# Attention scores of two head-pair units per pass over the TensorE array, and a new order of the steps of the first attention and of chunk 0

## The chip, the cores and the metric

One core of a Trainium2 chip runs the kernel. The metric is the time of one execution on the device in microseconds, the median over several runs. The engines are TensorE (PE, with its weight loads shown apart as PEld), VectorE (DVE), ScalarE (ACT), GpSimd (POOL) and SyncE (SP), which here only issues DMAs. Every engine works through its own queue in program order, and waits on semaphores for the others.

## What is computed

```python
scores = scale * q @ k.T                       # B=4, H=8, S=576, D=64
scores = where(mask[h], scores, -1e9)          # heads 0-3: window of 32; heads 4-7: window of 32 with stride 4
attn = exp(scores - max); attn /= sum + 1e-9
x = (attn @ v) as [2304, 512]
g = h - tanh(h),  h = x @ w_in                 # 512 -> 2048
x = g @ w_out                                  # 2048 -> 512
logits = x @ phi                               # 32 slots, 8 experts
slots = softmax over the tokens(logits).T @ x
out = softmax over the slots(logits) @ experts(slots)   # relu(slots @ w1) @ w2
```

## The kernel before, in words

The 2304 tokens are worked off in chunks of 512, `ch` 0 to 3, and a rest of 256. Each batch `b` of the attention gives the 512 tokens of chunk `b` and 64 of the rest.

**Attention.** The eight heads are four pairs (`PO = (2, 3, 0, 1)`: the two pairs with stride come first); each pair has three units `i`, so a batch has `NU = 12`. A unit holds two heads: head 0 in partitions 0 to 63 of q and k, head 1 in 64 to 127. A unit of a pair with stride has four blocks of 48 queries by 80 keys for each head, one of a plain pair three blocks of 64 by 96. A unit goes through `emit_scores` (PE: for batches 0 and 1 a bf16 matmul that writes the mask, then one f32 matmul for each block and head; DVE: the maximum, `L360`; ACT: the exponentials with their sums, `L363`), `emit_norm` (DVE: reciprocal, `L377`; POOL: the product, `L378`), `emit_trans` (PE: transposes, `L387`; ACT copies them out), `emit_pv` (PE: the product with v, `L408`; ACT copies the high part to `xhi`; DVE subtracts for the low part `xlo`, `L444`). An f32 matmul stands as two records in the trace, so the 84 score matmuls of a batch's 12 units are 168 records.

**Order.** The first attention (batch 0) runs alone, in an order that is sorted by numbers: unit `i` has the time `t = t0 + dt * i`, and its norm, transposes and product with v are put at `t` plus `NORM`, `TRANS` and `PV` times `dt`. The times only sort; nothing waits for them. Between the units stand conversions of weights, loads, and small `warm` matmuls. The attention of batch `b+1` is laid between the matmuls of chunk `b`, two units to a step.

**Chunk 0.** `mixed_step` runs eight times, `s` = 0 to 7. A step holds two blocks of 128 hidden columns, `a = 2s` and `b = 2s + 1`; each is twelve matmuls of 512 columns (`emit_h`, `L563` to `L565`), `tanh` on ACT (`L569`), the subtraction on DVE (`L572`), a transpose on DVE (`emit_gT`, `L585`) and logits on PE (`L578`). Between them the step converts further weights from 64-bit words (`conv_a` ACT `L496`; `conv_b` DVE `L504` and `L505`; `conv_in_c` ACT copy and POOL `L518`; `conv_out_c` PE `L526`, copies on ACT and DVE; `conv_out_d` PE `L537` and a copy on DVE to `cvb`), and carries the attention of batch 1 (`an`): `turn_qk` transposes a pair's q and k on DVE (`L260`, `L261`), in steps 0, 1, 2 and 4 (`QKS`), then `norms`, `trans`, `score`, `values`. The PSUM tiles `mm` are a ring of five; a PE group that takes one waits until the copy out of the tile five before it is done.

**Chunks 1 to 3** run `phase_step`, which has no conversions; chunks 1 and 2 carry batches 2 and 3, whose mask is added on DVE (`L357`). Then come the rest chunk, the slots, the experts and the output.

Of the kernel before, what the change touches and what calls it, by code (L numbers as in the profile page):

```python
# [31 lines left out]
MASKPE = 2  # L32
PO = (2, 3, 0, 1)
VB = (1, 2, 3)
# [10 lines left out]
NORM = (0.57, 0.28)  # L45
TRANS = (1.67, 1.76)
PV = (3.37, 3.39)
# [17 lines left out]
def moe_kernel(ctx: ExitStack, tc: tile.TileContext, q, k, v, w_in, w_out, phi, w1, w2, out):  # L65
# [258 lines left out]
    def emit_scores(b, i):  # L324
        p, u = PO[i // 3], i % 3
        nb, nq, nk = shape(i)
        ps = mm([128, nb, nk])
        mask = mask_d[:, (0, 4, 2)[u]:(4, 8, 6)[u]] if nb == 4 else mask_p[:, min(u, 1):min(u, 1) + 3]
        by_pe = b < MASKPE
        nr = nq if by_pe else 64  # L330
        if by_pe:
            nc.tensor.matmul(
                ps.rearrange("p c k -> p (c k)"), lhsT=id2.rearrange("p a k -> p (a k)"),
                rhs=mask[0:64].rearrange("p c k -> p (c k)"), start=True, stop=True,
            )
        for c in range(nb):
            for x in range(2):
                step = 1
                if nb == 4:

                    r2, qi = divmod(2 * u + c // 2, 3)
                    q0 = 288 * (c % 2) + 144 * r2
                    q0, k0 = q0 + nq * qi, q0 + max(0, nq * qi - 32)
                    if b in VB:
                        q0, k0 = (288 * (c % 2) + r2 + 2 * (t - 288 * (c % 2) - 144 * r2) for t in (q0, k0))
                        step = 2
                else:
                    q0, k0 = nq * (nb * u + c), max(0, nq * (nb * u + c) - 32)
                r = slice(64 * x, 64 * x + 64)
                nc.tensor.matmul(  # L350
                    ps[64 * x:64 * x + nr, c, :], lhsT=qT[b, p][r, q0:q0 + step * (nr - 1) + 1:step],
                    rhs=kT[b, p][r, k0:k0 + step * (nk - 1) + 1:step],
                    start=not by_pe, stop=True, skip_group_check=True,
                )
# [37 lines left out]
    def emit_pv(b, i):  # L392
# [5 lines left out]
        pt = sc_pt.pop((b, i))  # L398
        o = mm([128, 192])
        for n0 in range(nb):  # L400
            for hh in range(2):
                if nb == 4:
                    m, x = divmod(n0, 2)
                    r2, qi = divmod(2 * u + m, 3)
                    n, c, col = 3 * (2 * r2 + x) + qi, 2 * m + hh, 96 * x + nq * m
                else:
                    n, c, x, col = nb * u + n0, n0, hh, nq * n0
                nc.tensor.matmul(  # L408
                    o[64 * hh:64 * hh + 64, col:col + nq], lhsT=vt[b, p](n, hh),
                    rhs=pt[:, c, 64 * x:64 * x + nq], start=True, stop=True,  # L410
                )
# [34 lines left out]
        if b in VB:  # L446
            lows.append(low)
        else:
            low()
# [367 lines left out]
    class Attn:  # L817
# [19 lines left out]
        def score(self, i):  # L837
            if i < NU:
                emit_scores(self.b, i)
# [28 lines left out]
    with tc.manual_schedule():  # L868
# [7 lines left out]
        for b, (t0, dt) in enumerate((ATT0,)):  # L876
            for i in range(NU):
                t = t0 + dt * i
                at(t, emit_scores, b, i)
                at(t + NORM[b] * dt, emit_norm, b, i)  # L880
                at(t + TRANS[b] * dt, emit_trans, b, i)
                at(t + PV[b] * dt, emit_pv, b, i)
                if b == 0:
                    at(t + WAT * dt, warm, WARM if i < NWARM else 2)
            for p in range(NP):
# [5 lines left out]
        for t, f, *args in ((46.0, load_qk_blocks, 1, PO[0]), (50.0, load_v, 1, PO[0], nc.sync)):  # L891
            at(t, f, *args)
# [21 lines left out]
        for _, _, f, args in sorted(steps, key=lambda s: s[0:2]):  # L914
            f(*args)

# [13 lines left out]
        def mixed_step(an, ch, s, xh, xl, gs, posts):  # L930
# [7 lines left out]
            pa, gs[a] = emit_first(ch, xh, xl, a, first), gring.next()  # L938
            an.norms(s - 1)
            if 0 < s < 7:  # L940
                conv_a("in", 2 + a)
                conv_a("in", 2 + b)
            emit_tanh(pa, gs[a])
            if s == 0:
                conv_a("in", 2)
                conv_a("in", 3)
# [28 lines left out]
            an.score(2 * s)  # L975
            an.score(2 * s + 1)
# [10 lines left out]
        def phase_step(an, ch, s, xh, xl, gs, posts):  # L987

            a, b = 2 * s, 2 * s + 1
            pa, gs[a] = emit_h(xh, xl, a), gring.next()  # L990
            if an and s in QKS:
# [18 lines left out]
            if an:  # L1010
                an.trans(s)
                an.score(2 * s)
                an.score(2 * s + 1)
# [228 lines left out]
```

## Time and profile before

| | |
|---|---|
| median of 3 runs | 470.75 us (470.69 to 472.73) |
| profiled execution | 471.14 us, of which the trace spans 469.3 us |
| mean granted clock of TensorE in it | 0.976 of full speed |
| busy in the span: PE, DVE, ACT, POOL | 432.2, 250.8, 203.4, 83.8 us |
| first attention | about 5 to 62 us of the span |
| chunk 0 (`mixed_step`) | about 62 to 160 us |
| chunks 1 and 2 with batches 2 and 3 | about 160 to 310 us |

The trace gives, for each engine, when each group of instructions began, how long it took, how long the engine stood idle before it and on what. "mm<-qk 64*64 64x96" is a matmul into the tile `mm` from the tile `qk` with a 64 by 64 stationary and a moving operand of 64 partitions by 96 columns. A granted clock of 1.00 is 2.4 GHz, 0.50 is 1.2 GHz.

### The profile page before, as it was taken

To read this page: it belongs to the slowest core of one execution; us is meant where nothing else is said; L and a number is where in the kernel's file an instruction comes from. 1 tells how busy PE (TensorE), PEld (TensorE's weight loads), DVE (VectorE), ACT (ScalarE), POOL (GpSimd) and SP (SyncE) were. 2 spreads that over 40 slices of the span, in tenths; PEclk is the share of its full clock that TensorE was granted. 3 is DMA by queue.
4 is the path that set the end of the run, shared out by engine and by line. 5 is a ranking of instruction groups with operands and counts; after the bars stand their busy time and mean duration, and the time that the engine had idled before them with its cause. 6 is when DMAs were issued, how large, how long until landed. Compare 5 with 4: busy or idle time off the path is not lost.

```text
span 469.3 us, 11363 instructions
## 1 busy us (share of the span) xinstructions
PE 432.2 (92%) x4567; PEld 315.6 (67%) x4567; DVE 250.8 (53%) x605; ACT 203.4 (43%) x701; POOL 83.8 (18%) x99
## 2 busy tenths in 40 slices
PE   6989877999898999999999999999999999999980
PEld 4766646877677775887775788776777689645330
DVE  1455658578965775756475776453644251233041
ACT  4777436677664272654253455322212223213131
POOL 3321414334235040223031031100000000010000
PEclk9999899799999999999999999999999999999996
DMA  8998986889564202163423111167000799899938
GB/s 235 232 264 232 288 119 219 216 257 266 187 118 82 55 14 41 45 84 52 85 54 54 39 40 24 68 226 314 1 1 17 253 352 400 327 403 410 407 123 314
DMA packets 102021, 81.16 MB, mean 173 GB/s; under 512 B 78032, under 2 KB 81872, under 8 KB 101968
## 3 DMA queue, kind: packets, MB, share of 16 engines
q1 hardware_dynamic: 101968, 80.43, 57.6%
q8 instruction: 36, 0.59, 0.5%
q14 instruction: 17, 0.14, 0.1%
HBM read 71.50 MB, written 8.91 MB: 171 GB/s over the span
## 4 chain that ended last, share of the span: by engine, by line
PE 61%; issue 12%; DVE 11%; ACT 10%; DMA 3%; POOL 0%; DVEq 0%; SPq 0%; ACTq 0%; POOLq 0%
PE h L563 11%; PE h L564 10%; PE h L565 10%; PE mm L350 5%; PE lg L578 4%; PE mm L408 4%; ACT mem L363 3%; PE h L786 3%; PE y L811 3%; PE mm L702 3%; PE mm L387 2%; ACT mem L569 1%; DMA wo_dram<-cva 1%; DVE cva L505 1%; PE warm L205 1%
## 5 line engine op out<-in xcount | busy, mean ns | idle before, releaser
L563 PE MATMUL h<-xhi,wts 128*128 128x512 f32 x256 | 106.8, 417 | 0.4 <-ACT xhi L103 0.4
L564 PE MATMUL h<-xlo,wts 128*128 128x512 f32 x256 | 101.4, 396 | 0.0
L565 PE MATMUL h<-xhi,wts 128*128 128x512 f32 x256 | 100.9, 394 | 0.0
L569 ACT ACTIVATE mem<-h 128x512 f32<-128x512 f32 x72 | 42.9, 596 | 122.9 <-PE h L565 115.5
L572 DVE TENSOR_TENSOR mem<-h,mem 128x512 f32<-128x512 f32 x72 | 49.4, 686 | 86.5 <-ACT mem L569 86.4
L378 POOL TENSOR_TENSOR mem<-mem 128x320 f32<-128x320 f32 (+1 forms) x48 | 33.3, 703 | 169.9 <-DVE mem L377 108.6
L563 PEld LDWEIGHTS h<-xhi,wts 128*128 128x128 f32 x256 | 49.1, 192 | 16.5 <-issue 5.9
L565 PEld LDWEIGHTS h<-xhi,wts 128*128 128x128 f32 x256 | 48.8, 191 | 11.0
L564 PEld LDWEIGHTS h<-xlo,wts 128*128 128x128 f32 x256 | 49.2, 192 | 9.0 <-DVE xlo L444 0.3
L585 DVE STREAM_TRANSPOSE gt<-mem 128x512 f32<-128x512 f32 x64 | 41.1, 684 | 0.0
L350 PEld LDWEIGHTS mm<-qk 64*64 64x64 f32 (+1 forms) x672 | 27.7, 133 | 18.0 <-issue 9.2
L350 PE MATMUL mm<-qk 64*64 64x96 f32 (+2 forms) x672 | 34.5, 246 | 4.8 <-DVE qk L261 2.9
L363 ACT ACTIVATE mem<-mem 128x80 f32<-128x80 f32 (+1 forms) x84 | 29.7, 355 | 15.7 <-DVE mem L360 15.7
L363 ACT ACTIVATE mem<-mm,mem 128x80 f32<-128x80 f32 (+1 forms) x84 | 26.7, 331 | 13.1 <-DVE mem L360 13.0
L103 ACT COPY mem<-mm 96x384 f32<-96x384 f32 (+4 forms) x64 | 26.0, 435 | 8.7 <-PE mm L387 7.1
L408 PE MATMUL mm<-mem,v 80*64 80x48 f32 (+1 forms) x672 | 27.0, 230 | 2.3 <-ACT mem L103 1.7
L408 PEld LDWEIGHTS mm<-mem,v 80*64 80x64 f32 (+1 forms) x672 | 22.9, 142 | 7.4 <-ACT mem L103 2.5
L578 PE MATMUL lg<-mem 128*32 128x128 f32 x576 | 26.5, 285 | 0.9 <-DVE mem L572 0.9
L387 PE MATMUL mm<-mem 112*80 112x112 f32 (+1 forms) x168 | 22.8, 270 | 2.4 <-POOL mem L378 1.2
L578 PEld LDWEIGHTS lg<-mem 128*32 128x32 f32 x576 | 15.1, 111 | 11.8 <-issue 9.2
L702 PE MATMUL mm<-gt,mem 32*32 32x512 f32 x512 | 19.9, 597 | 1.3 <-DVE xlo L444 1.3
L387 PEld LDWEIGHTS mm<-mem 112*80 112x80 f32 (+1 forms) x168 | 16.2, 122 | 6.7 <-issue 3.7
(178 smaller groups left out, 630.5 us busy)
## 6 DMA issues: line engine op xcount, KB each, us to landing
ex<-in_moe_w_dram SPq DMA_DIRECT2D x21, 1024.0 KB, 11.0
gt<-in_moe_w_out_dram SPq DMA_DIRECT2D x7, 1024.0 KB, 7.3
gt<-in_moe_w_in_dram SPq DMA_DIRECT2D x7, 1024.0 KB, 7.4
gt<-in_moe_w_dram SPq DMA_DIRECT2D x6, 1024.0 KB, 9.9
mem<-in_moe_w_dram SPq DMA_DIRECT2D x5, 1024.0 KB, 6.9
wo_dram<-cva SPq DMA_DIRECT2D x16, 256.0 KB, 6.4
wo<-wo_dram SPq DMA_DIRECT2D x4, 1024.0 KB, 7.6
out_dram<-o SPq DMA_DIRECT2D x8, 512.0 KB, 4.8
```

Source lines behind the costliest of these rows:

```text
L350: nc.tensor.matmul(ps[64 * x:64 * x + nr, c, :], lhsT=qT[b, p][r, q0:q0 + step * (nr - 1) + 1:step], rhs=kT[b, p][r, k0:k0 + step * (nk - ...
L363: nc.scalar.activation(out=pr[:, c, :], in_=ps[:, c, :], func=ACTF.Exp, bias=nm[:, c:c + 1], accum_out=sm[:, c:c + 1],)
L387: nc.tensor.transpose(ps[:, c, :], pr[0:P, c, :], ident[0:P, 0:P])
L408: nc.tensor.matmul(o[64 * hh:64 * hh + 64, col:col + nq], lhsT=vt[b, p](n, hh), rhs=pt[:, c, 64 * x:64 * x + nq], start=True, stop=True,)
L563: nc.tensor.matmul(ps, lhsT=wh, rhs=xh[:, kt, :], start=(n == 0), stop=False)
L564: nc.tensor.matmul(ps, lhsT=wh, rhs=xl[:, kt, :], start=False, stop=False)
L565: nc.tensor.matmul(ps, lhsT=wl, rhs=xh[:, kt, :], start=False, stop=(n == KT - 1))
L569: nc.scalar.activation(out=g, in_=ps, func=ACTF.Tanh)
L572: nc.vector.tensor_tensor(out=g, in0=ps, in1=g, op=ALU.subtract)
L578: nc.tensor.matmul(lgs[ch][32 * j:32 * j + 32, 0:128], lhsT=wp[:, ft, :], rhs=g[:, 128 * j:128 * j + 128], start=(ft == 0), stop=(ft == NF ...
L585: nc.vector.transpose(out=gt[:, ft, :], in_=g)
L702: nc.tensor.matmul(tp[fq][32 * x:32 * x + 32, :], lhsT=z["dT"][r, x, j, :], rhs=gt[r, :, 128 * j + 32 * x:128 * j + 32 * x + 32], start=(j ...
```

## The change

Three things change.

1. `emit_scores` takes any number of units. In `mixed_step` and `phase_step` it gets two: the score matmuls of both units alternate, and the second unit's heads are written to the other half of the partitions (`y = x ^ sw`, `tile_position=(64 * x, 64 * y)`), so that the four 64 by 64 quarters of the array are all used. `emit_pv` reads the exchanged halves back (`x ^ sw`). The maxima and exponentials of both units are emitted behind the scores of both. In the first attention `emit_scores` still gets one unit.
2. In the first attention, `NORM`, `TRANS` and `PV` of batch 0 change, the subtraction for `xlo` is put off until behind the next unit's maximum, and a load of `w_in` stands ahead of the first loads of batch 1's q and k.
3. In `mixed_step`, `turn_qk` and `emit_gT` move up to stand directly behind the matmuls of block `a`, around `norms`; the two `conv_a("in")` move behind `tanh` of block `a` (for `s > 0`).

```diff
-NORM = (0.57, 0.28)
-TRANS = (1.67, 1.76)
-PV = (3.37, 3.39)
+NORM = (1.02, 0.28)
+TRANS = (1.75, 1.76)
+PV = (2.6, 3.39)
...
+    def emit_scores(b, *units):
...
+            if len(work):
+                swapped.add((b, i))
+            work.append((p, u, nb, nq, nk, nr, by_pe, ps, mask, len(work)))
+        for c in range(work[0][2]):
+            for p, u, nb, nq, nk, nr, by_pe, ps, mask, sw in work:
+                for x in range(2):
+                    step, y = 1, x ^ sw
...
+                    r = slice(64 * x, 64 * x + 64)
+                    nc.tensor.matmul(
+                        ps[64 * y:64 * y + nr, c, :], lhsT=qT[b, p][r, q0:q0 + step * (nr - 1) + 1:step],
+                        rhs=kT[b, p][r, k0:k0 + step * (nk - 1) + 1:step],
+                        start=not by_pe, stop=True, skip_group_check=True, tile_position=(64 * x, 64 * y),
+                    )
+        for i, (p, u, nb, nq, nk, nr, by_pe, ps, mask, sw) in zip(units, work):
+            emit_exps(b, i, ps, mask, by_pe)
...
-                    rhs=pt[:, c, 64 * x:64 * x + nq], start=True, stop=True,
+                    rhs=pt[:, c, 64 * (x ^ sw):64 * (x ^ sw) + nq], start=True, stop=True,
...
-        if b in VB:
-            lows.append(low)
-        else:
-            low()
+        lows.append(low)
...
                 at(t, emit_scores, b, i)
+                at(t, emit_lows)
...
-        for t, f, *args in ((46.0, load_qk_blocks, 1, PO[0]), (50.0, load_v, 1, PO[0], nc.sync)):
+        for t, f, *args in ((50.0, load_qk_blocks, 1, PO[0]), (52.0, load_v, 1, PO[0], nc.sync)):
...
             pa, gs[a] = emit_first(ch, xh, xl, a, first), gring.next()
+            if s in QKS:
+                turn_qk(an.b, PO[QKS.index(s)])
             an.norms(s - 1)
+            if s == 0:
+                conv_a("in", 2)
+                conv_a("in", 3)
+            else:
+                for n in (a - 2, a - 1):
+                    emit_gT(ch, n, gs[n])
+            emit_tanh(pa, gs[a])
             if 0 < s < 7:
                 conv_a("in", 2 + a)
                 conv_a("in", 2 + b)
-            emit_tanh(pa, gs[a])
...
             if s < 7:
                 conv_b("in", 2 + a)
                 conv_in_c(2 + a)
-            if s in QKS:
-                turn_qk(an.b, PO[QKS.index(s)])
-            if s < 7:
                 conv_b("in", 2 + b)
                 conv_in_c(2 + b)
-            if s:
-                for n in (a - 2, a - 1):
-                    emit_gT(ch, n, gs[n])
...
-            an.score(2 * s)
-            an.score(2 * s + 1)
+            an.score(2 * s, 2 * s + 1)
```

VectorE's queue in step 1 of chunk 0, before, from the subtraction of block `a` to that of block `b` (L260 and L261 are `turn_qk`, L585 the two `emit_gT`, the last copy that of `conv_out_d`):

```order
L572 TENSOR_TENSOR mem<-h,mem 128x512
L103 COPY cvb<-mm 128x512
L504 TENSOR_SCALAR cvb<-cvb 128x512
L505 SCALAR_TENSOR_TENSOR cvb<-gt,cvb 128x512
L260 STREAM_TRANSPOSE qk<-rqk 128x576
L261 STREAM_TRANSPOSE qk<-rqk 128x576
L504 TENSOR_SCALAR mem<-mem 128x512
L505 SCALAR_TENSOR_TENSOR mem<-gt,mem 128x512
L585 STREAM_TRANSPOSE gt<-mem 128x512 x2
L103 COPY cvb<-mm 128x128 x2
L572 TENSOR_TENSOR mem<-h,mem 128x512
```

The same piece of the same queue after the change, from `turn_qk`, which now opens it:

```order
L260 STREAM_TRANSPOSE qk<-rqk 128x576
L261 STREAM_TRANSPOSE qk<-rqk 128x576
L391 RECIPROCAL mem<-mem 128x4 x2
L596 STREAM_TRANSPOSE gt<-mem 128x512 x2
L583 TENSOR_TENSOR mem<-h,mem 128x512
L103 COPY cvb<-mm 128x512
L515 TENSOR_SCALAR cvb<-cvb 128x512
L516 SCALAR_TENSOR_TENSOR cvb<-gt,cvb 128x512
L515 TENSOR_SCALAR mem<-mem 128x512
L516 SCALAR_TENSOR_TENSOR mem<-gt,mem 128x512
L103 COPY cvb<-mm 128x128 x2
L583 TENSOR_TENSOR mem<-h,mem 128x512
```

The four transposes now stand ahead of the subtraction of block `a`, and nothing but the conversions is left between it and the copies of `conv_out_d`.

TensorE's queue in step 4 of chunk 0 around the scores, before (L332 is the mask, L350 the scores of one unit):

```order
L537 MATMUL mm<-cvb,mem 32x128 x8
L387 MATMUL mm<-mem 96x128 x6
L332 LDWEIGHTS mem
L332 MATMUL mm<-mem 128x288
L350 MATMUL mm<-qk 64x96 x6
L332 LDWEIGHTS mem
L332 MATMUL mm<-mem 128x288
L350 MATMUL mm<-qk 64x96 x6
L408 MATMUL mm<-mem,v 64x64 x12
```

And after:

```order
L548 MATMUL mm<-cvb,mem 32x128 x8
L401 MATMUL mm<-mem 96x128 x6
L337 LDWEIGHTS mem
L337 MATMUL mm<-mem 128x288
L337 LDWEIGHTS mem
L337 MATMUL mm<-mem 128x288
L359 MATMUL mm<-qk 64x96 x12
L422 MATMUL mm<-mem,v 64x64 x12
```

Both masks now stand ahead of the scores of both units, which are one run of twelve matmuls.

VectorE's queue in the first attention around units 7 and 8, before (L360 a unit's maximum, L444 the low part, L375 and L377 its norm):

```order
L360 TENSOR_REDUCE mem<-mm 128x3
L103 COPY cvb<-mm 128x512
L444 TENSOR_TENSOR xlo<-mm,xhi 128x2x96
L375 TENSOR_SCALAR mem<-mem 128x3
L377 RECIPROCAL mem<-mem 128x3
L103 COPY cvb<-mm 128x128
L504 TENSOR_SCALAR cva<-cva 128x512
L505 SCALAR_TENSOR_TENSOR cva<-gt,cva 128x512
L360 TENSOR_REDUCE mem<-mm 128x3
```

And after, the piece that begins with the same kind of row:

```order
L374 TENSOR_REDUCE mem<-mm 128x3
L458 TENSOR_TENSOR xlo<-mm,xhi 128x2x2x48
L389 TENSOR_SCALAR mem<-mem 128x3
L391 RECIPROCAL mem<-mem 128x3
L103 COPY mem<-mm 128x64
L374 TENSOR_REDUCE mem<-mm 128x3
```

The norm behind a maximum was that of the same unit; now it is that of the unit before it, and the low part stands directly behind the maximum.

## Rows read from the trace of the kernel before

**Rows 1.** Busy time by stretch: length, PE, PEld, DVE, ACT, POOL; clock, DMA, GB/s.

```profile
12.00:48.00 36.00, 32.67 (x447) 24.23 (x444) 19.49 (x62) 28.16 (x113) 8.89 (x15) 1.00 1.04 244
62.00:147.00 85.00, 74.59 (x750) 57.95 (x750) 63.29 (x142) 55.18 (x183) 30.43 (x29) 0.94 0.71 186
172.00:330.00 158.00, 156.24 (x1748) 117.30 (x1748) 95.37 (x233) 68.96 (x269) 24.35 (x29) 1.00 0.33 84
67.70:71.40 3.70, 3.70 (x32) 2.59 (x31) 2.48 (x6) 2.76 (x7) 2.07 (x2) 0.58 0.01 4
82.40:88.70 6.30, 6.30 (x69) 4.92 (x69) 3.95 (x10) 6.08 (x26) 3.56 (x4) 0.50 0.63 187
```

**Rows 2.** TensorE's waits from 62 to 172 us, and its two longest idle times.

```profile
PE mm L332 <- DVE cvb L103: 6.2, 5, 2.8
PE mm L350 <- DVE qk L261: 2.9, 1, 2.9
PE mm L408 <- ACT mem L103: 1.3, 1, 1.3
...
66.99 0.77 PE L350 MATMUL mm<-qk 64*48 64x80 f32 x16 [2.89 <-DVE qk L261]
82.40 0.42 PE L332 MATMUL mm<-mem 64*128 64x320 bf16 x1 [2.85 <-DVE cvb L103]
```

**Rows 3.** VectorE's timeline in chunk 0: start, length, instruction, idle before it.

```profile
62.08 0.29 DVE L444 TENSOR_TENSOR xlo<-mm,xhi 128x144 fp32r<-128x144 f32 x1
65.50 0.77 DVE L260 STREAM_TRANSPOSE qk<-rqk 128x576 f32<-128x576 f32 x1
66.20 0.73 DVE L261 STREAM_TRANSPOSE qk<-rqk 128x576 f32<-128x576 f32 x1
80.87 1.30 DVE L585 STREAM_TRANSPOSE gt<-mem 128x512 f32<-128x512 f32 x2
91.44 0.69 DVE L572 TENSOR_TENSOR mem<-h,mem 128x512 f32<-128x512 f32 x1 [4.17 <-ACT mem L569]
```

**Rows 4.** Steps 0 and 1: POOL's low weights, then ScalarE's tanh, conversions, exponentials.

```profile
66.32 1.27 POOL L518 TENSOR_TENSOR wts<-cvb,wts 128x512 fp32r<-128x512 f32 x1 [8.41 <-ACT wts L103]
...
69.16 0.59 ACT L569 ACTIVATE mem<-h 128x512 f32<-128x512 f32 x1
69.64 1.25 ACT L496 ACTIVATE cva<-gt 128x512 f32<-128x512 f32 x2
70.90 0.33 ACT L363 ACTIVATE mem<-mm,mem 128x80 f32<-128x80 f32 x1
...
74.97 0.59 ACT L569 ACTIVATE mem<-h 128x512 f32<-128x512 f32 x1
```

**Rows 5.** The chain that ended last, chunk 1: start, length, group.

```profile
177.21 4.41 PE mm L702 x115
186.04 1.29 PE mm L350 x32
187.33 1.07 PE mm L408 x32
195.60 1.14 PE mm L350 x24
```

**Rows 6.** The first attention: timeline of VectorE, POOL, SP and TensorE.

```profile
35.83 0.36 DVE L444 TENSOR_TENSOR xlo<-mm,xhi 128x192 fp32r<-128x192 f32 x1 [1.41 <-ACT xhi L103]
36.71 0.67 POOL L378 TENSOR_TENSOR mem<-mem 128x288 f32<-128x288 f32 x1 [3.20 <-DVE mem L377]
37.21 0.46 DVE L360 TENSOR_REDUCE mem<-mm 128x3 f32<-128x288 f32 x1 [0.67 <-PE mm L350]
37.26 3.68 SPq L243 DMA_DIRECT2D rqk<-in_k_dram  x4
46.59 0.63 PE L350 MATMUL mm<-qk 64*64 64x96 f32 x10
50.04 0.45 DVE L360 TENSOR_REDUCE mem<-mm 128x3 f32<-128x288 f32 x1
```

More of the change, by code (lines that the diff above doesn't have):

```diff
@@ L322, in shape @@
         return (4, 48, 80) if PO[i // 3] >= NP // 2 else (3, 64, 96)
-    def emit_scores(b, i):
-        p, u = PO[i // 3], i % 3
-        nb, nq, nk = shape(i)
[L327 to L343, printed above, removed]
-                    if b in VB:
-                        q0, k0 = (288 * (c % 2) + r2 + 2 * (t - 288 * (c % 2) - 144 * r2) for t in (q0, k0))
-                        step = 2
-                else:
[L348 to L354, printed above, removed]
@@ new lines, in moe_kernel @@
+    swapped = set()
+    def emit_scores(b, *units):
+        work = []
+        for i in units:
+            p, u = PO[i // 3], i % 3
+            nb, nq, nk = shape(i)
+            ps = mm([128, nb, nk])
+            mask = mask_d[:, (0, 4, 2)[u]:(4, 8, 6)[u]] if nb == 4 else mask_p[:, min(u, 1):min(u, 1) + 3]
+            by_pe = b < MASKPE
+            nr = nq if by_pe else 64
+            if by_pe:
+                nc.tensor.matmul(
+                    ps.rearrange("p c k -> p (c k)"), lhsT=id2.rearrange("p a k -> p (a k)"),
+                    rhs=mask[0:64].rearrange("p c k -> p (c k)"), start=True, stop=True,
+                )
[6 more added lines that the diff above has]
+                    step, y = 1, x ^ sw
+                    if nb == 4:
+                        r2, qi = divmod(2 * u + c // 2, 3)
+                        q0 = 288 * (c % 2) + 144 * r2
+                        q0, k0 = q0 + nq * qi, q0 + max(0, nq * qi - 32)
+                        if b in VB:
+                            q0, k0 = (288 * (c % 2) + r2 + 2 * (t - 288 * (c % 2) - 144 * r2) for t in (q0, k0))
+                            step = 2
+                    else:
+                        q0, k0 = nq * (nb * u + c), max(0, nq * (nb * u + c) - 32)
+                    r = slice(64 * x, 64 * x + 64)
+                    nc.tensor.matmul(
+                        ps[64 * y:64 * y + nr, c, :], lhsT=qT[b, p][r, q0:q0 + step * (nr - 1) + 1:step],
+                        rhs=kT[b, p][r, k0:k0 + step * (nk - 1) + 1:step],
+                        start=not by_pe, stop=True, skip_group_check=True, tile_position=(64 * x, 64 * y),
+                    )
+        for i, (p, u, nb, nq, nk, nr, by_pe, ps, mask, sw) in zip(units, work):
+            emit_exps(b, i, ps, mask, by_pe)
@@ L355, in emit_scores, with emit_exps @@
+    def emit_exps(b, i, ps, mask, by_pe):
+        nb, nq, nk = shape(i)
         pr = prs.next()[:, 0:nb * nk].rearrange("p (c k) -> p c k", c=nb)
@@ L397, in emit_pv @@
             xlo[b] = unit("xlo", [128, KT, 512], F32R)
-        pt = sc_pt.pop((b, i))
+        pt, sw = sc_pt.pop((b, i)), (b, i) in swapped
         o = mm([128, 192])
@@ L444, in low @@
                 nc.vector.tensor_tensor(out=f(lo), in0=src, in1=f(hi).bitcast(F32), op=ALU.subtract)
-        if b in VB:
-            lows.append(low)
-        else:
-            low()
+        lows.append(low)
     lows = []
@@ L835, in trans, with score @@
                     emit_trans(self.b, i)
-        def score(self, i):
-            if i < NU:
-                emit_scores(self.b, i)
+        def score(self, *units):
+            if units[0] < NU:
+                emit_scores(self.b, *units)
         def values(self, s):
@@ L884, in moe_kernel @@
                     at(t + WAT * dt, warm, WARM if i < NWARM else 2)
+            for i in range(NU, NU + 3):
+                at(t0 + dt * i, emit_lows)
             for p in range(NP):
@@ L915, in moe_kernel @@
             f(*args)
+        emit_lows()
         cst = {}
@@ L938, in mixed_step @@
             pa, gs[a] = emit_first(ch, xh, xl, a, first), gring.next()
+            if s in QKS:
+                turn_qk(an.b, PO[QKS.index(s)])
             an.norms(s - 1)
+            if s == 0:
+                conv_a("in", 2)
+                conv_a("in", 3)
+            else:
+                for n in (a - 2, a - 1):
+                    emit_gT(ch, n, gs[n])
+            emit_tanh(pa, gs[a])
             if 0 < s < 7:
@@ L942, in mixed_step @@
                 conv_a("in", 2 + b)
-            emit_tanh(pa, gs[a])
-            if s == 0:
-                conv_a("in", 2)
-                conv_a("in", 3)
             emit_sub(pa, gs[a])
@@ L990, in phase_step @@
             pa, gs[a] = emit_h(xh, xl, a), gring.next()
+            if s == 2:
+                emit_lows()
             if an and s in QKS:
@@ L1011, in phase_step @@
                 an.trans(s)
-                an.score(2 * s)
-                an.score(2 * s + 1)
+                an.score(2 * s, 2 * s + 1)
                 an.values(s)
```

## The prediction

> **What bounds the kernel now.** I read the busy time by stretch first, since the share of the whole span (432 of 469 us on TensorE) mixes stages with different limits [rows 1]. From 172 to 330 us TensorE is busy 156.24 of 158 us at full clock: there a microsecond of TensorE is a microsecond of the kernel. From 62 to 147 us, the seven steps of chunk 0 that carry attention or conversions, it is busy 74.59 of 85 us, and its granted clock is 0.94: 10.4 us of waiting, and 0.06 of 85 us, about 5.1 us, lost to the clock. From 12 to 48 us, the body of the first attention, it stands idle only 3.3 of 36 us, at full clock.
>
> Next I read what TensorE waited for in chunk 0 [rows 2]. All of it is other engines: 6.2 us in five waits of a mask matmul for a copy on VectorE (`conv_out_d`), 2.9 us of step 0's scores for `turn_qk`, 1.3 us once, in step 6, for ScalarE. No DMA stands there. The two long waits, 2.89 us before 66.99 and 2.85 us before 82.40, are followed by the two stretches at low clock [rows 1]: 3.7 us at 0.58 from 67.70, 6.3 us at 0.50 from 82.40. By the same work at full clock these cost 3.7 x 0.42 = 1.55 us and 6.3 x 0.50 = 3.15 us, 4.7 together. That is nearly all of the 5.1 us, so the shorter waits, which share out the other 3.4 us of the 6.2 and the 1.3, cost no clock.
>
> Last, VectorE's own rows [rows 3]: before the subtraction of block a in step 2 it stood idle for 4.17 us, waiting for tanh, while four transposes that were ready (`turn_qk` 0.77 + 0.73, the two `emit_gT` 1.30) stood behind it in the queue, ahead of the copy for which TensorE then waited.
>
> **The scores in four quarters.** Now a pair of units with stride takes 1.29 us for 32 records and a plain pair 1.14 us for 24 [rows 5]: 40.3 and 47.5 ns each, two quarters at a time. What four quarters give, this trace shows for no 64 by 64 tile. The nearest row is the group that uses the whole array in 32 by 32 tiles, rows and columns at once: 115 records in 4.41 us. The code issues 128 there (some records are missing), so 34.5 ns each, though 512 columns shared by sixteen tiles would need less. The product with v, two column halves and only 48 columns wide, costs 33.4 ns a record (1.07 us for 32) [rows 5]. Both say that below about 34 ns something other than columns sets the pace, and I take 34. A batch has 96 records with stride and 72 plain, so it gives back 96 x 6.3 + 72 x 13.5 ns = 1.6 us. The bounds: if only the columns counted, a record would cost half of now, 20 and 24 ns, and a batch would give back 3.6 us; if two quarters stay the limit, nothing. Batches 2 and 3 lie in the stage where TensorE is the bound: **3.2 us** (0 to 7.2). Batch 1 lies in chunk 0, where I count its **1.6 us** too, as TensorE sets most of its steps once the waits go.
>
> The Trainium skill (TensorEngine Tiling (Array Packing), Instruction Overhead) gives each matmul an overhead of about 60 cycles, whatever its width below that; at 2.4 GHz that is an estimate of 25 ns, and by it a batch would give back some 3.1 us in place of 1.6. The trace's two narrow groups at 33 to 35 ns are slower than that, and I go by them.
>
> The later start of the first unit's maximum (both units' scores now end together) costs nothing in chunks 1 and 2, where VectorE is busy 95 of 158 us.
>
> **Chunk 0, step by step.** `turn_qk` can begin in step 0 once the last low part is done, at 62.08 + 0.29 = 62.37, and takes 1.43 us [rows 3]: 63.8. TensorE was there at 66.99 - 2.89 = 64.1, so the 2.89 us go. But the next block's third matmul needs low weights that POOL finishes at 66.32 + 1.27 = 67.59 [rows 4], and the conversion ahead of them is no earlier, as `turn_qk` now stands before it instead of behind. Two masks, 32 records at 34 ns and eight of logits bring TensorE to about 65.9; it may begin two matmuls (0.46 us) ahead of 67.59. So 1.2 us of waiting come back.
>
> In step 1, ScalarE's order rules. Its second tanh of step 0 stood at 69.16, held by the second conversion on VectorE; without `turn_qk` between the conversions that is 1.4 us earlier, about 67.8. Then follow the two `conv_a`, 1.25 us, and the exponentials (from 70.90, with tanh at 74.97 behind them and two more `conv_a`) [rows 4]. These last 3 us and are not shortened, so tanh of block a comes at about 72.2. VectorE still has the reciprocals and 1.30 us of `emit_gT` ahead of its subtraction, which ends near 75.1, and the copy that `conv_out_d` needs near 75.7. TensorE, which started this step at 67.1 and needs some 6.4 us to get there, waits from 73.5: 2.2 us. About 0.8 us more fall to the second mask and the product with v. So step 1 keeps about 3.0 us of waiting for the 2.85 that it had; it moves, to other instructions.
>
> In steps 2 to 5 the queue order does what it is for: about 3 us of ready work fill VectorE's wait for tanh, the copies of `conv_out_d` come 1.3 us (or, with `turn_qk`, 2.8) sooner relative to tanh, and the waits there, 3.4 us, mostly go; I leave 0.6. VectorE then has 11 to 11.5 us of work in a step with `turn_qk` against 11.5 to 12 on TensorE, so little more than this can be kept up. Step 6 has neither scores nor `turn_qk`: its 1.3 us stay.
>
> Waiting in chunk 0: 10.4 before; 1.2 + 3.0 + 0.6 + 1.3 = 6.1 after; **4.3 us** won. Clock: the wait of 1.2 us in step 0 is no longer than the one of step 6, which cost no clock, so 1.55 us come back; the 2.2 us in step 1 lie between those and the 2.85 that did cost it, and I count half of 3.15. **3.1 us** (1.5 to 4.7).
>
> `conv_a` behind tanh costs nothing as long as VectorE reaches `conv_b` later: the subtraction, low parts and a copy, some 1.8 us, stand between.
>
> **The first attention.** The change takes from VectorE's queue the waits for ScalarE that hold a unit's maximum back: the scores of the last unit were issued at 46.59, its maximum began at 50.04 [rows 6]. But TensorE has a new wait. The transposes of unit i-1 now need a norm that stands behind the maximum of unit i: maximum 0.46, low part and norm 0.88 (35.83 to POOL's start at 36.71), POOL 0.67, with hops some 2.1 us after the scores end [rows 6]. Ahead of those transposes TensorE has 1.5 to 2.3 us of other work. With transposes (0.5), mask and scores (0.9) the loop is at least 3.5 us a unit, and TensorE's scores came every 3.4 to 3.6 us before. So the body gains nothing; the earlier last maximum is mostly eaten by a conversion that now stands ahead of the last norm. I take **0.5 us** (-2 to 3).
>
> On SP a store that waits for VectorE and a megabyte load move ahead of batch 1's first q and k, which were issued until 37.26 + 3.68 = 40.9 [rows 6] and turned at 65.50 [rows 3]: over 20 us of cover, and the delay is a few. The loads of `w_out` in chunk 0 wait for `conv_b`, which comes sooner too.
>
> **Sum.** 3.2 + 1.6 + 4.3 + 3.1 + 0.5 = 12.7 us. From the profiled execution's 471.14 us that is 458.4; the median of the runs lies 0.4 lower, so **458.0 us**. What follows chunk 0 waits for TensorE and shifts with it.
>
> **Rivals.**
> - *Serial quarters (slower).* Two tiles of the same row half, or two row halves that write one PSUM bank, might have to take turns. A matmul alone would then cost about its pair's time now, 80 and 95 ns, twice as much: a batch would lose 96 x 40.3 + 72 x 47.5 ns = 7.3 us, three 21.9 instead of winning 4.8, and the kernel would take about 485. It decides from some 59 ns a record, 16 above the present mean, where 504 records eat the other 7.9 us that the sum wins. Against it: today's pairs write one bank from both row halves, and the sixteen-tile group runs four row groups and four column groups at 34.5 ns [rows 5]. Chance 0.04. The Trainium skill (TensorEngine Tiling (Array Packing), Restrictions and Gotchas) states this rule: row tiles cannot access the same PSUM bank at once. The present pace, which is under a full column time for each matmul, speaks against it here.
> - *Columns are the pace.* 20 and 24 ns a record: 6 us more, 452. For it: nothing narrow; 0.15.
> - *No more than two quarters at once.* The scores give nothing, 462.8; 0.13.
> - *ScalarE and VectorE become the bound of chunk 0.* VectorE is busy 63 and ScalarE 55 of 85 us there; if their order keeps the waits and the low clock, only the clock of step 0 and the scores are won, 465; 0.15.
> - *The first attention gets longer* by its new wait, 0.5 us in six units: 461.5; 0.1.
>
> **Chances.** The forecast's own case, 453 to 463, has 0.43. The range 450 to 465 leaves out the serial case and the outermost of the others, near 2 in 10. About 0.5% (2.4 us) is what a measurement can tell here; only the serial case, or several losses together, end above 468.4. Faster 0.91, same 0.04, slower 0.05.
>
> **What would show it.** Scores at about 34 ns a record in chunks 1 and 2 (a pair of units in 1.1 and 0.8 us); no wait for `turn_qk` in step 0 but one for the low weights; a wait at `conv_out_d` in step 1; the waits of masks for copies gone in steps 2 to 5; full clock after step 0. Wrong would be: scores over 45 ns a record, mask waits still there, or the last maximum of the first attention no earlier and its transposes waiting for POOL.

## The result and the profile after

The changed kernel takes 454.96 us (median of 4 runs, 454.54 to 455.33) against 471.13 us (470.69 to 472.73) for the kernel before in the same job: 0.9651 of it, 95% interval 0.9625 to 0.9676. The forecast was 458.0 us, range 450 to 465. The profiled execution took 455.33 us, with a span of 453.4 us.

I divide both spans at three instructions that each trace has: the first tanh of chunk 0, the first tanh of step 7 (behind the mixed steps), and the first matmul into `y`.

| stretch | before, us | after, us | change | forecast |
|---|---|---|---|---|
| start to chunk 0's first tanh | 63.20 | 64.97 | +1.77 | -0.5 |
| from there to step 7's first tanh | 88.28 | 78.47 | -9.81 | -9.0 (1.6 + 4.3 + 3.1) |
| from there to the first `y` | 284.81 | 276.79 | -8.02 | -3.2 |

So the total came within 3.4 us of the forecast's sum by luck: the last stretch won 4.8 us more than I said, the first lost 2.3 us more, and the two errors stand against each other. In the middle row, too, the terms are off and only their sum is near, as the experiments show.

The page of the changed kernel, busy time and granted clock (tenths, 40 slices):

```profile
PE 418.4 (92%) x4567; PEld 303.4 (67%) x4567; DVE 246.7 (54%) x605; ACT 203.5 (45%) x701; POOL 84.2 (19%) x99
...
PEclk9999889999999999999999999999999999999996
```

Busy time by stretch after, columns as in [rows 1]. The second row holds the half-clock stretch ahead of chunk 0; the third answers to the row of 62 to 147 us there; the fourth is the table's second stretch, and the last row is the same stretch of the kernel before; the fifth row answers to that of 172 to 330 us:

```profile
12.00:48.00 36.00, 31.23 (x429) 23.29 (x427) 19.06 (x61) 28.01 (x111) 9.26 (x16) 1.00 1.03 242
54.00:62.00 8.00, 8.00 (x40) 5.95 (x40) 1.85 (x7) 1.11 (x4) 3.54 (x3) 0.58 0.76 178
62.00:147.00 85.00, 77.33 (x854) 58.26 (x853) 64.54 (x152) 57.75 (x189) 35.11 (x31) 1.00 0.80 202
64.97:143.44 78.47, 70.82 (x798) 53.85 (x797) 61.86 (x144) 55.14 (x185) 35.11 (x31) 1.00 0.80 207
170.00:320.00 150.00, 148.83 (x1675) 112.25 (x1657) 96.26 (x235) 66.08 (x252) 22.91 (x28) 1.00 0.34 88
...
63.20:151.48 88.28, 77.87 (x798) 60.83 (x797) 63.59 (x142) 56.12 (x186) 34.45 (x31) 0.94 0.72 184
```

Chunk 0 has full clock in this profile, where it had 0.94; TensorE still idles 78.47 - 70.82 = 7.65 us in the mixed steps (88.28 - 77.87 = 10.41 before). TensorE's waits from 58 to 165 us, total, times, longest, which answer to [rows 2]:

```profile
PE mm L422 <- ACT mem L103: 2.8, 5, 1.3
PE mm L337 <- DVE cvb L103: 2.3, 4, 0.8
PE h L574 <- ACT wts L103: 1.0, 1, 1.0
PE mm L537 <- DVE cva L516: 0.8, 2, 0.5
PE h L576 <- POOL wts L529: 0.8, 1, 0.8
```

The wait for `turn_qk` is gone, and no mask waits longer than 0.8 us, where the longest was 2.85. VectorE's timeline shows why: the transposes of `turn_qk` (L260, L261) begin in step 0 at 64.26 instead of 65.50 [rows 3], and in step 2 `turn_qk` and `emit_gT` stand ahead of the subtraction (L583), which then follows at once; the next one waits 0.79 us for tanh. Before, VectorE stood idle for 4.17 us ahead of step 2's first subtraction [rows 3], with this ready work behind it in the queue. After the change:

```profile
64.26 0.77 DVE L260 STREAM_TRANSPOSE qk<-rqk 128x576 f32<-128x576 f32 x1
...
84.45 0.77 DVE L260 STREAM_TRANSPOSE qk<-rqk 128x576 f32<-128x576 f32 x1
85.15 0.73 DVE L261 STREAM_TRANSPOSE qk<-rqk 128x576 f32<-128x576 f32 x1
85.92 1.27 DVE L596 STREAM_TRANSPOSE gt<-mem 128x512 f32<-128x512 f32 x2
87.12 0.65 DVE L583 TENSOR_TENSOR mem<-h,mem 128x512 f32<-128x512 f32 x1
...
92.20 0.69 DVE L583 TENSOR_TENSOR mem<-h,mem 128x512 f32<-128x512 f32 x1 [0.79 <-ACT mem L580]
```

The chain that ended last, chunk 1, which answers to [rows 5], with blocks of 32 score records (some are missing) and of 24:

```profile
152.99 0.75 PE mm L359 x31
...
175.83 0.74 PE mm L359 x29
...
184.84 0.66 PE mm L359 x24
```

1.29 us became 0.75 and 1.14 became 0.66: 23.4 and 27.5 ns a record, not 34. By these lengths a batch (three blocks of each kind) gives back 3 x 0.54 + 3 x 0.48 = 3.1 us in place of my 1.6; what the kernel gets of it is measured below.

The first attention paid for its new order. TensorE's timeline, where its transposes (L401) wait for POOL's normalisation (L359 are the scores of the last two units):

```profile
43.59 0.53 PE L401 MATMUL mm<-mem 128*96 128x128 f32 x3 [0.56 <-POOL mem L392]
44.64 0.71 PE L359 MATMUL mm<-qk 64*64 64x96 f32 x12
...
47.80 0.53 PE L401 MATMUL mm<-mem 128*96 128x128 f32 x3 [0.82 <-POOL mem L392]
48.48 0.71 PE L359 MATMUL mm<-qk 64*64 64x96 f32 x12
...
52.42 0.53 PE L401 MATMUL mm<-mem 128*96 128x128 f32 x3 [1.83 <-POOL mem L392]
```

The last scores began at 48.48 (46.59 before [rows 6]), and the last maximum at 49.83 (50.04 before): it did come sooner after its scores, but the scores came later, and it is only 0.2 us earlier in all.

### The profile page after: what moved, and what is told of

Read it like the earlier page. It is cut to its first block, busy times and chain, and to the rows that moved or that the text cites. A ratio compares the mean times of both kernels' runs of the same rounds, so it can differ in the third digit from the quotient of the medians.

```text
span 453.4 us, 11355 instructions
## 1 busy us (share of the span) xinstructions
PE 418.4 (92%) x4567; PEld 303.4 (67%) x4567; DVE 246.7 (54%) x605; ACT 203.5 (45%) x701; POOL 84.2 (19%) x99
## 4 chain that ended last, share of the span: by engine, by line
PE 56%; DVE 13%; issue 13%; ACT 9%; SPq 3%; POOL 2%; DMA 2%; POOLq 0%; DVEq 0%; ACTq 0%
PE h L574 10%; PE h L575 9%; PE h L576 9%; ACT mem L377 4%; PE h L797 3%; PE lg L589 3%; PE y L822 3%; PE mm L713 3%; PE mm L359 3%; PE mm L401 3%; PE mm L422 3%; SPq L241 2%; DMA raww<-in_moe_w_out_dram 2%; DVE mem L374 2%; DVE gt L596 1%
## 5 line engine op out<-in xcount | busy, mean ns | idle before, releaser
L583 DVE TENSOR_TENSOR mem<-h,mem 128x512 f32<-128x512 f32 x72 | 49.2, 683 | 73.8 <-ACT mem L580 73.7
L377 ACT ACTIVATE mem<-mem 128x80 f32<-128x80 f32 (+1 forms) x84 | 29.7, 355 | 15.9 <-DVE mem L374 15.9
L377 ACT ACTIVATE mem<-mm,mem 128x80 f32<-128x80 f32 (+1 forms) x84 | 26.8, 332 | 10.9 <-DVE mem L374 10.9
L401 PE MATMUL mm<-mem 112*80 112x112 f32 (+1 forms) x168 | 23.6, 274 | 5.8 <-POOL mem L392 5.5
L359 PEld LDWEIGHTS mm<-qk 64*64 64x64 f32 (+1 forms) x672 | 17.7, 131 | 9.7 <-issue 6.8
L401 PEld LDWEIGHTS mm<-mem 112*80 112x80 f32 (+1 forms) x168 | 16.0, 123 | 11.2 <-POOL mem L392 7.8
L359 PE MATMUL mm<-qk 64*64 64x96 f32 (+2 forms) x672 | 23.2, 245 | 0.2 <-ACT qk L316 0.2
L250 POOL TENSOR_SCALAR rqk<-rqk 128x576 f32<-128x576 f32 x12 | 19.7, 1652 | 0.0
```

The costliest lines, as they stand in the source:

```text
L359: nc.tensor.matmul(ps[64 * y:64 * y + nr, c, :], lhsT=qT[b, p][r, q0:q0 + step * (nr - 1) + 1:step], rhs=kT[b, p][r, k0:k0 + step * (nk - ...
L377: nc.scalar.activation(out=pr[:, c, :], in_=ps[:, c, :], func=ACTF.Exp, bias=nm[:, c:c + 1], accum_out=sm[:, c:c + 1],)
L401: nc.tensor.transpose(ps[:, c, :], pr[0:P, c, :], ident[0:P, 0:P])
L583: nc.vector.tensor_tensor(out=g, in0=ps, in1=g, op=ALU.subtract)
```

## The experiments

**One part at a time.** `e1_quarters`, `e2_chunk0` and `e3_first` are the kernel before with one of the three parts of the change each: the scores in four quarters, the new order of `mixed_step`, the new order of the first attention. `e4_oldfirst` is the changed kernel without the last. (`phase_step` got one more line, `emit_lows()`, which none of the three parts holds; it has its own experiment below.)

> The kernel before with the scores of two units in four quarters, and nothing else of the change. If a score record costs 24 ns (80 columns) and 27 ns (96), as the trace of the changed kernel shows, a batch gives back 3.0 us: 6.0 us in chunks 1 and 2, and 0 to 3 in chunk 0, where the waits for VectorE stay; 462 to 465 us, ratio 0.981 to 0.987. If the price of 34 ns of the prediction held without the new order, 3.2 to 4.8 us, 466 to 468 us. If the four quarters only pay together with the new order, no change.

> The kernel before with the new order of chunk 0's steps alone. If the order removes the waits and the low clock by itself, chunk 0 gets 6 to 8 us shorter (4.7 of them clock), 463 to 465 us, ratio 0.983 to 0.987. Rival: what VectorE is relieved of only moves the waits to other instructions, as the prediction had it for step 1, and the clock falls again after a wait of some 2 us there: 3 to 4 us, 467 to 468 us.

> The kernel before with the new order of the first attention alone. If that order costs what the two traces differ by until the first tanh of chunk 0, 1.8 us, it gives 472.9 us, ratio 1.004. If the prediction's 0.5 us gain holds and the 1.8 us come from elsewhere, 470.6 us, ratio 0.999.

> The changed kernel with the first attention in its old order. If the new order of the first attention is a loss, this is 1.8 us faster than the changed kernel, about 453.2 us, ratio to the kernel before 0.962, and faster than both. If chunk 0 begins with what must wait anyway (batch 1's q and k from memory, low weights from POOL), the 1.8 us come back as a wait there: 455 us, ratio 0.965.

| kernel | us | of before, 95% interval | chunk 0's mixed steps, us | step 7 to `y`, us |
|---|---|---|---|---|
| before | 471.94 | | 88.28 | 284.81 |
| e1_quarters | 468.34 | 0.9927 (0.9900 to 0.9955) | 90.96 | 279.71 |
| e2_chunk0 | 462.42 | 0.9792 (0.9765 to 0.9819) | 78.15 | 284.82 |
| e3_first | 472.87 | 1.0031 (1.0015 to 1.0046) | 88.10 | 284.82 |
| e4_oldfirst | 452.80 | 0.9601 (0.9577 to 0.9625) | 78.14 | 276.83 |

(The last two columns are of each profiled execution.) `e1_quarters` came out above the 466 to 468 us expected with 34 ns a record, `e2_chunk0` a little below its 463 to 465. Chunk 0's gain is the order's alone: 10.1 us with it and without the quarters, 10.1 with both. (Ten of these kernels have the new order; in eight profiles of them the mixed steps take 78.1 to 78.5 us, in `e5_nolows` 79.0, in `e8_halfcols` 80.7, both with a stretch of low clock from about 80 us on.) Which of the moves in that order gave how much, no run tells. The faster scores make nothing there faster. In `e1_quarters` chunk 0 even gets longer: TensorE comes sooner to waits that don't move, its mask waits grow from 6.2 to 9.3 us, and behind one that grew from 1.07 to 1.77 us the clock falls a third time, to 0.52 from 98.4 to 104.6 us. Its waits and its mixed steps:

```profile
PE mm L337 <- DVE cvb L103: 9.3, 5, 3.8
PE mm L359 <- DVE qk L261: 2.8, 1, 2.8
...
62.91:153.87 90.96, 77.15 (x798) 59.60 (x797) 63.94 (x142) 56.39 (x186) 34.61 (x31) 0.91 0.72 181
```

In `e2_chunk0`, the mixed steps:

```profile
64.75:142.90 78.15, 74.43 (x798) 57.54 (x797) 62.14 (x143) 54.94 (x184) 35.05 (x31) 1.00 0.77 205
```

TensorE idles 3.72 us there, and 7.65 after the whole change: the 3.6 us of matmul time that the quarters saved became waiting, and 0.3 us besides. Both profiles show these steps at full clock, in 78 us. The first attention's new order loses: `e3_first` is slower than before by 0.3%, and without it the changed kernel is faster than either kernel.

**What made the scores faster.** Both edits are in `emit_scores`:

```
# e6_samequarters: two units in turn, in the old two quarters
-            if len(work):
-                swapped.add((b, i))
...
-                    step, y = 1, x ^ sw
+                    step, y = 1, x
# e7_roworder: the same half of the rows twice in a row
-            for p, u, ... in work:
-                for x in range(2):
+            for x in range(2):
+                for p, u, ... in work:
```

> The changed kernel with its scores still issued in turn from two units, but both units in the same two quarters of the array. If the number of quarters sets the price of a record, records go back to 40 ns (80 columns) and 47 ns (96 columns), each of batches 2 and 3 costs 3.0 us more, and the time is 461.0. Rival: the turn between units (another accumulator after every pair) or the mask matmuls put ahead is what made the records faster: records stay at 24 to 27 ns and the time at 455.0.

> The changed kernel with the two loops inside a block exchanged: the four quarters are still used in turn, but two records in a row have the same half of the rows. If only the number of quarters at work counts, 24 and 27 ns a record and 455.0 us stay. Rival: a weight load runs beside a running matmul only when the two lie in different halves of the rows (the Trainium skill, TensorE: Matmul & The Clock Gate, has such a rule); then every second record waits for its load. The trace has the same records with one quarter less to overlap at 40 and 47 ns, so at most 16 to 20 ns on half of the 168 records of a batch: up to 1.5 us for each of batches 2 and 3, 458.0 us.

Measured: `e6_samequarters` 460.85 us, 0.9763 (0.9742 to 0.9784); `e7_roworder` 455.35 us, 0.9655 (0.9632 to 0.9678). The chain of `e6_samequarters` in chunk 1 has the old lengths:

```profile
177.50 1.30 PE mm L357 x32
187.04 1.14 PE mm L357 x24
```

From the first scores of chunk 1 to `y` it needs 5.6 us more than the changed kernel (272.84 against 267.24), two batches at 2.8 us. The quarters do it, not the turn between units. By `e1_quarters`, which lacks the added `emit_lows()`, they give 284.81 - 279.71 = 5.1 us. Both are less than the 6.2 us of the chain's lengths; a part of the difference is that TensorE now comes to the rest matmuls sooner and waits there for ScalarE's tanh, 0.53 and 0.59 us, where it did not before. In `e7_roworder` the stretch is 267.2 us and its score groups have the same busy time to 0.1 us: the order of row halves does not matter here, and the rule of the Trainium skill that its expectation names has no effect that this kernel shows.

**How a record's time depends on its columns.** `e8_halfcols` multiplies half of the key columns in batches 2 and 3 only:

```
-    ps[64 * y:64 * y + nr, c, :], lhsT=...
-    rhs=kT[b, p][r, k0:k0 + step * (nk - 1) + 1:step],
+    ps[64 * y:64 * y + nr, c, 0:nk if by_pe else nk // 2], lhsT=...
+    rhs=kT[b, p][r, k0:k0 + step * ((nk if by_pe else nk // 2) - 1) + 1:step],
...
```

> The changed kernel, but in batches 2 and 3 each score matmul computes only the first half of its key columns, and VectorE adds the mask to that half taken twice, so VectorE's work stays as it is. If a record costs its column time divided by the quarters at work and some 7 ns on top (66.7 and 80 ns by four, plus 7), records of 40 and 48 columns take 15 and 17 ns; with 96 and 72 of them in a batch that is 1.5 us a batch, 451.9 us in all. Rival: 24 to 27 ns is a floor for one record whatever its columns: 455.0 us. (The estimate of the Trainium skill, TensorE: Matmul & The Clock Gate, of about 60 cycles for each matmul, 25 ns, would say the same as this rival.)

Measured: 454.01 us, 0.9619 (0.9597 to 0.9642), 1.3 us less than `e7_roworder` in the same job; from chunk 1's first scores to `y` 265.8 us. Chain, chunk 1:

```profile
176.21 0.62 PE mm L359 x32
185.13 0.49 PE mm L359 x24
```

Neither expectation holds: 0.62 us a block where 0.48 (15 ns) or 0.75 was expected, that is 19.4 ns a record, and 20.4 with 48 columns. One reading that fits the lengths: a block costs some 0.2 us once, and each record half as much in four quarters as in two. From 1.29 = 32r + f and 0.75 = 16r + f, r is 33.8 ns in two quarters and 16.9 in four, f 0.21 us; from the plain blocks, 1.14 and 0.66, r is 40 and 20 ns, f 0.18. The rates stand nearly as 80 to 96 columns do. With half the columns the same f leaves 13 ns for 40 and for 48 columns, not 8.5 and 10, which looks like a floor. This split is fitted to two lengths with two unknowns, and no run shows it by itself. That f is nearly one record's own length (238 ns is the mean of the 80-column group) suggests the end of the block's last record; no run tested that either.

**The line that I overlooked.** `phase_step` of the changed kernel issues `emit_lows()` behind the first `h` of step 2. `e5_nolows` leaves that out:

```
-            if s == 2:
-                emit_lows()
```

> The changed kernel without the added line of phase_step that issues the deferred low parts behind the first h of its third step. If the line spares chunk 1 and chunk 2 a wait each (in the trace of before the first rest matmul of the deferred rows waits 1.29 us for VectorE's low part, once in each chunk, and the quarters alone gave 5.1 us in these chunks where the whole change gave 8.0), the time goes up by 2.6 to 2.9 us, to about 457.7, and the trace shows the two waits of 1.3 us for the low part again. Rival: the 2.9 us come from elsewhere in these chunks, and the line is worth nothing: 455.0, and no such wait.

Measured: 458.99 us, 0.9725 (0.9705 to 0.9745). TensorE's timeline of `e5_nolows`, rest matmuls of the deferred rows in chunk 1:

```profile
168.42 1.05 PE L713 MATMUL mm<-gt,mem 32*32 32x512 f32 x6 [0.53 <-ACT mem L677]
169.90 4.41 PE L713 MATMUL mm<-gt,mem 32*32 32x512 f32 x122 [0.43 <-DVE xlo L458]
```

and of the changed kernel:

```profile
166.93 4.46 PE L713 MATMUL mm<-gt,mem 32*32 32x512 f32 x128 [0.53 <-ACT mem L677]
```

Without the line TensorE stops after six of 128 records for VectorE's low part: from the first start to the last end 5.89 us instead of 4.46, twice in the kernel. From chunk 1's first scores to `y` it takes 270.13 us against 267.24: 2.9 us, as expected. `e7_roworder`, which keeps the line and ran in the same job, is 3.6 us faster. The other 0.7 us or so are not the line's: they lie in the mixed steps, where the code is the same (79.03 us against 78.25), and there the profile of `e5_nolows` has 0.58 of the clock from 82 to 86 us, that of `e7_roworder` full clock.

**Where the first attention loses.** `e9_normearly` is the changed kernel with `NORM` of the first batch back at 0.57; `e10_lownow` issues that batch's low parts at once again; `e12_lowdefer` is `e4_oldfirst` with the low parts deferred as in the changed kernel. The edits of the first two:

```
-NORM = (1.02, 0.28)      # e9_normearly
+NORM = (0.57, 0.28)
...
-        lows.append(low)      # e10_lownow
+        if b in VB:
+            lows.append(low)
+        else:
+            low()
```

> The changed kernel with NORM of the first batch back at 0.57; the deferred low parts, the earlier value products and the later transposes stay. If the transposes wait for POOL because the normalisation is now issued behind the next unit's scores (3.7 us of waits in the first attention after the change, 0.5 us before), these waits fall below 1 us and the time comes to that of the changed kernel with the old first attention, 0.960 of before (452.8 us). Rival: the deferred low parts or the value products in front of the transposes cost the 2.2 us: 0.9645 to 0.966 (455.0) stays.

> The changed kernel with the first batch's low parts issued at once, as in before; NORM, TRANS and PV stay as changed. If the late normalisation alone makes the waits for POOL, they stay at some 3.7 us and the time stays at 0.9645 to 0.966 of before (455.0 us) or goes up, since the low parts then stand ahead of the maxima on VectorE again (up to 0.4 us in each of 12 units if nothing hides it). Rival: the deferral is what costs, and the time falls to 0.960 (452.8 us).

> The changed kernel with the old first attention (0.960 of before, 452.8 us), but with the first batch's low parts deferred behind the next unit's scores. If the deferral does what it looks like, VectorE takes a unit's maximum up to 0.4 us earlier, and where the maximum bounds a unit (the scores follow each other at 4 us) the first attention shortens by up to 1 us: 0.958 to 0.960. Rival: the maximum waits for its scores anyway (VectorE is idle 0.67 us ahead of the one at 37.2 us in the trace of before), and nothing changes: 0.960; or the low parts come too late for the rest matmuls: above 0.961.

Measured in one job: 453.46 us, 0.9622 (0.9602 to 0.9642); 455.44 us, 0.9651 (0.9627 to 0.9676); 453.09 us, 0.9597 (0.9569 to 0.9625). TensorE's waits from 8 to 56 us, changed kernel:

```profile
PE mm L401 <- POOL mem L392: 5.5, 8, 1.8
```

`e10_lownow`:

```profile
PE mm L401 <- POOL mem L392: 4.4, 5, 2.4
```

In `e9_normearly` there is no such row; 0.5 us of another wait for POOL and 4 us of short waits for ScalarE and VectorE stand in its place. So the late normalisation makes the wait, and the deferral of the low parts is worth nothing that can be measured either way. By the medians `e9_normearly` wins back some 1.5 of the 2.2 us that `e4_oldfirst` wins; its interval overlaps with those of both, so the split between `NORM` and the rest (`TRANS`, `PV`, two loads) stays open. The best versions, `e4_oldfirst` and `e12_lowdefer`, can't be told apart.

**The clock alone.** `e11_warm` is the kernel before, with idle matmuls in its two long waits of chunk 0:

```
+            warm(12 if s == 0 else 0)
             an.score(2 * s)
+            warm(11 if s == 1 else 0)
             an.score(2 * s + 1)
```

> The kernel before, with idle matmuls (128x256, results unused) put on TensorE into its two long waits of chunk 0: 24 of them ahead of the first scores of step 0 (the wait of 2.9 us that ends at 66.99 us) and 22 ahead of the second scores of step 1 (the wait of 2.85 us that ends at 82.40 us). The order of everything else and the waits themselves stay. If the clock falls because TensorE stands still there, the two stretches at half clock behind the waits go, 4.7 us come back, and the time is 466.3 us, 0.990 of before; that is then the clock's part of the 10 us that the new order of chunk 0 gains. Rival: the clock falls for another reason and the stretches stay: 471, or some tenths more where the idle matmuls run past the end of the waits.

Measured: 470.11 us, 0.9949 (0.9931 to 0.9968). Its windows over the two stretches and chunk 0:

```profile
66.00:74.00 8.00, 7.64 (x78) 5.96 (x77) 6.71 (x12) 4.86 (x15) 4.16 (x3) 1.00 0.09 12
80.00:90.00 10.00, 9.38 (x122) 7.52 (x121) 8.02 (x17) 7.54 (x29) 5.82 (x5) 1.00 0.84 260
62.00:147.00 85.00, 77.75 (x833) 60.39 (x833) 63.84 (x143) 55.77 (x184) 31.23 (x29) 1.00 0.70 183
```

The clock no longer falls in the two stretches, so the standstill did make it fall there; the mean granted clock is 0.982 to 0.986 in all six runs, and at most 0.977 in the eleven of the kernel before. But of the 4.7 us only about half came back: the mixed steps take 86.01 us instead of 88.28, and the median is neither the 466.3 us expected nor the rival's 471. ScalarE's tanh rows show where the 1.55 us of the first stretch went; the last row is the first tanh of the kernel before, the others of which stand in [rows 4]:

```profile
64.98 0.60 ACT L569 ACTIVATE mem<-h 128x512 f32<-128x512 f32 x1 [1.27 <-PE h L565]
70.94 0.59 ACT L569 ACTIVATE mem<-h 128x512 f32<-128x512 f32 x1
76.78 0.58 ACT L569 ACTIVATE mem<-h 128x512 f32<-128x512 f32 x1
...
63.20 0.60 ACT L569 ACTIVATE mem<-h 128x512 f32<-128x512 f32 x1 [1.28 <-PE h L565]
```

From the first tanh to the third are 11.80 us, and 11.77 in the kernel before (63.20, 69.16 and 74.97): so here ScalarE and VectorE set the pace, and TensorE at half clock was still in time. (The idle matmuls ran some 0.3 us past the end of the first wait, too little to be the missing 2.4.) From this kernel to `e2_chunk0`, both at full clock, the mixed steps fall by 7.9 us.

`e4_oldfirst` shows the same from the other side. Its profile has half clock from 68.0 to 71.2 us, behind waits of 0.96 and 0.81 us, and its mixed steps take 78.14 us all the same:

```profile
66.00:70.00 4.00, 2.77 (x7) 1.96 (x8) 2.79 (x6) 3.53 (x11) 3.56 (x3) 0.73 0.71 85
70.00:74.00 4.00, 4.00 (x21) 3.31 (x20) 3.93 (x10) 3.94 (x18) 1.33 (x2) 0.84 0.20 30
```

## Why the forecast came out near, step by step

**Scores, 3.2 us in chunks 1 and 2: too small, the step that failed most.** "Both say that below about 34 ns something other than columns sets the pace" was a floor taken from groups with another layout: sixteen tiles of 512 columns, and two column halves of 48. Neither bounds a 64 by 64 tile in four quarters, which took 23.4 and 27.5 ns. (The first group was misread besides: TensorE issues six of its 128 records ahead of a wait, so the 4.41 us belong to 122, 36 ns each; and with 512 columns it is not a narrow group.) The rival "columns are the pace" has the rate right if the split above holds, 17 and 20 ns against 34 and 40; what it missed is then the 0.2 us a block that do not halve. Batches 2 and 3 gave 5.1 us by `e1_quarters` and 5.6 by `e6_samequarters`, between my 3.2 and that rival's 7.2. The estimate by the Trainium skill's 60 cycles (TensorEngine Tiling (Array Packing), Instruction Overhead), 3.1 us a batch, agrees with the chain's lengths. But the prediction put the page's 25 ns for a matmul on a record, and a matmul is two records here: put on a record it is no floor, as `e8_halfcols` shows 19.4 and 20.4 ns, and put on a matmul it leaves an estimate of 12.5 ns a record, which none of these rows contradicts. The number was near by luck. The serial quarters are refuted by every trace with four quarters. The rule of the same page's Restrictions and Gotchas on row tiles and one bank is not borne out either: each unit writes one bank from both row halves, and its records of 80 columns take 40 ns in two quarters and 23 in four, where a record of 112 columns that has the array to itself takes 111 ns (L387, a transpose, in the chain of before):

```profile
185.14 0.89 PE mm L387 x8
```

**Missing from the sum: the added `emit_lows()`, 2.9 us.** [rows 5] begin with the 115 records that start behind the wait it removes; I used that row for a price and did not ask what stood ahead of it. The prediction put the line at nothing by leaving it out.

**Scores, 1.6 us in chunk 0: wrong.** They gave nothing there (`e2_chunk0` and `e4_oldfirst`, 78.15 and 78.14 us). "TensorE sets most of its steps once the waits go" was the mistake: VectorE and ScalarE set them, and TensorE waits longer (7.65 us of idle time with the quarters, 3.72 without). That much of the rival "ScalarE and VectorE become the bound" came true; its low clock did not.

**Waits, 4.3 us, and clock, 3.1 us: the queue order did what was foretold; the sizes were off, and the two are not separate.** `turn_qk` no longer holds step 0; waits of 0.96 and 0.81 us for converted weights stand there, 1.8 us where 1.2 were foretold, as ScalarE's copy holds a matmul beside POOL. Step 1 keeps 1.9 us in four pieces (0.34, 0.50, 0.76, 0.33), not 3.0. None of them is near the 2.85 that cost the clock, and it is full here for the whole of the mixed steps; but that the shorter waits cost no clock, on which the prediction's 3.1 us rest, does not hold in general: it fell behind the first two in `e4_oldfirst`, and behind the same four in `e5_nolows` and `e8_halfcols`. Order alone brings idle time from 10.41 to 3.72 us, 6.7 won. Clock alone brings 2.3 us net (`e11_warm`), not 3.1 or 4.7. Both together, as `e2_chunk0` has them, bring 10.1 us, against 7.4 in the sum; that 9.8 us stand against 9.0 in the table is these 2.7 us too few, the scores' 1.6 too many, and the 0.3 us of added waiting.

**First attention, +0.5 us forecast: wrong in sign.** The wait that the prediction named as new came, at 0.23 to 0.82 us a unit and 1.83 at the end, and `e4_oldfirst` shows what the whole part costs: 0.9601 against 0.9651 of before, some 2.4 us. On the kernel before it costs less, 0.9 to 1.5 us (`e3_first`). "So the body gains nothing" took the loop's bound of 3.5 us for its length; the scores came every 3.84 us instead (44.64 to 48.48, and 38.42 us for the ten steps from 10.06), against 36.07 us for the same ten steps before, 10.52 to 46.59. So the body lost 2.35 us. The rival "the first attention gets longer" was right in its wait; the loss lies between its 3 us and the term's bound of -2. The 1.77 us of the two profiles mixes it with the length of the half-clock stretch at 54 to 62 us, which differs from one profile to the next.

## What to carry to other kernels

Ask of each saved microsecond whether its engine sets the pace of that stage: the same quarters were worth 5.1 to 5.6 us where TensorE was the bound and nothing in chunk 0, where queue order alone was worth 10. A floor for an instruction's time may be taken from another group only if that group has the same tiling; else keep the wider bound as the forecast's middle. And when work is moved behind a later one to free a queue, count the path of whoever consumes the moved work, hops included: the new order of the first attention, with its late normalisation, cost some 2 us for a last maximum that came 0.2 us sooner.

## What was not expected of the hardware

The same steps can run at full clock in one kernel's profile and not in another's: chunk 0 of `e5_nolows` and of the changed kernel are the same code with waits within 0.5 us of each other, yet the one has 0.58 of the clock from 82 to 86 us and the other 1.00 throughout. That is more than one profile's chance: in all four runs of `e5_nolows` the mean clock is 0.977 to 0.978, in those of the changed kernel 0.981 to 0.985. No run shows the reason. At 54 to 58 us every other profile of these kernels shows 0.50 to 0.74, and that of `e8_halfcols` 1.00. A microsecond or two between two profiles here is the clock's, so I let the medians and the stretches at full clock decide. And a wait of 2.9 us ahead of a slowed stretch may cost only itself: 1.5 us of half clock behind the first one vanished into another engine's time, and so did the 3.2 us at half clock in `e4_oldfirst`.
